# Inverse token norm held as 96 x 3 and spread by matmul, in a Nystrom attention followed by two MLPs

## The chip, the cores and the metric

One core of a Trainium2 chip runs the whole program. The metric is the device time of one execution in microseconds (us). The core has five engines that each work through their own instructions in order: TensorE (PE, its weight loads listed as PEld), VectorE (DVE), ScalarE (ACT), GpSimd (POOL) and SyncE (SP), which here issues nearly all DMAs.

## The reference

```python
def _attn_ref(q, k, v):                       # B, H, S, D = 4, 8, 576, 64
    q_lm, k_lm = ...                          # means over 18 neighbours: 32 landmarks
    A, Bm, C = sm(q, k_lm), sm(q_lm, k_lm), sm(q_lm, k)
    Z = Bm.T / (norm1 * norminf + 1e-06)
    for _ in range(6):
        Z = 2 * Z - Z @ Bm @ Z
    return A @ Z @ C @ v

def _moe_ref(x, w_gate, w_val, w_out, rms_g): # 2304 tokens, 512 -> 1536 -> 512
    rms = np.sqrt(np.mean(x * x, axis=-1, keepdims=True) + 1e-06)
    xn = x / rms * rms_g
    g = xn @ w_gate
    return g * (1 / (1 + np.exp(-g))) * (xn @ w_val) @ w_out

def _moe2_ref(x, w_in, w_out, s, b):          # 512 -> 2048 -> 512
    r = np.maximum(x @ w_in, 0.0)
    return (s * (r * r) + b) @ w_out
```

The attention's output, 512 features for each of 2304 tokens, is what `_moe_ref` calls `x`. The change touches only how `1 / rms` is formed and laid out.

## The kernel before, in words

The work is cut by batch: four batches of 576 tokens, each in two halves `hf` of `HC` = 288 tokens. For each batch `attention(b, ...)` makes the attention's factors; `fused`, `hidden` and `out_mm` then run the first MLP over twelve column blocks of its weights; the second MLP follows for all tokens at the end, from about 530 us. The first batch's attention is all that can run at the start. The attention of each later batch is spread among the MLP work of the batch before it. The int64 weights of the first MLP are loaded, narrowed to float32 on ACT and DVE by `narrow` (lines 897 to 904) and written back once in float32 during the first batch; later batches read that copy.

The order of instructions is fixed before the run by `Scheduler.run`, a planner that walks over all operations with a cost for each and a key (its due time), and gives each to an engine at the planned moment. An operation may name several engines: a pair of costs from `dp(n)` offers `t_dve(n)` on DVE and `t_pool(n)` on POOL, and within the attention an extra `SPA` = 0.5 us counts against DVE. The planner's cost of `t_dve(288)` is 0.36 us, of `t_pool(288)` 0.75 us. Once written, each engine's order is kept, whatever the real durations are. While the planner sees PE free in the first 60 planned us it fills the time with dummy matmuls (`warm`, line 1228).

The norm of a half works as follows. `x_mm` (line 821) makes the 512 features of 288 tokens in four pieces of 128 partitions by 288 tokens in PSUM, ACT squares each into `xq` with the scale 512^-0.5 (line 827), and, in later batches, two additions fold the four pieces into one (line 833). A matmul with a 128 x 128 matrix of ones (line 839) sums over the partitions and leaves the same sum in all 128 rows of `pS`: 128 x 288. The first batch accumulates its four pieces in four such matmuls instead of folding them. On `pS`, in place in PSUM, DVE adds 1e-6 (line 843) and takes the reciprocal (line 844), ACT takes the square root (line 847, for which ACT changes its table, and changes it back for the next Tanh at line 1006), and DVE multiplies the two tiles `a` of the half by it (line 852). ACT and POOL then split `a` into a high and a low part `xh`, `xl` (lines 856 and 858), the moving operand of every first matmul of that batch (line 991).

Around it, on the same engines, stands the MLP's own loop: PE makes `pU` (line 972), ACT and DVE split it into `uh`, `ul` (lines 978 and 980), PE multiplies by `xh`, `xl` (line 991), ACT takes Tanh (line 1006), and DVE makes the hidden values (lines 1008 and 1012), which free the PSUM tiles that the next line 972 and line 991 write. PE's output matmuls are lines 1035 and 1039, their operands split at lines 871 to 873.

In PSUM the later batches' attention has two banks (`at_r`), the first batch's seven (`any_r`).

Of the kernel before, what the change touches and what calls it, by code (L numbers as in the profile page):

```python
# [13 lines left out]
ACTF = mybir.ActivationFunctionType  # L14
ALU = mybir.AluOpType
# [207 lines left out]
def t_dve(n):  # L223
    return 0.065 + 0.00104 * n
# [6 lines left out]
def t_act(n):  # L231
    return 0.055 + 0.00085 * n
# [10 lines left out]
def t_mm4(n):  # L243
    return 0.00167 * max(n, 120)
# [3 lines left out]
def tile_nystrom_attention_two_mlps(  # L248
# [152 lines left out]
    def attention(b, t0, t1):  # L401
# [8 lines left out]
        def at(alts, pos, fn, r=(), w=(), pair=False):  # L410
            mine.append(op(alts, 0.0, fn, r, w, pair or set(alts) == {"dve", "pool"}))
            mine[-1].spare = {"dve": SPA if b else SPA0}
            if not first and "sp" not in mine[-1].alts:
                mine[-1].after = RELB
            at_ops.append(mine[-1])

        def dp(n):
            return {"dve": t_dve(n), "pool": t_pool(n)}
# [389 lines left out]
        for hf in range(2):  # L808
            p0 = 0.7 + 0.15 * hf
            xq = Buf(t_ring)  # L810
            n_mine = len(mine)
            for c in range(KD):
                g, pr = divmod(c, 2)
                if pr == 0:
                    pX2 = [Buf(ps_r), Buf(ps_r)]
                pX = pX2[pr]

                def x_mm(_, g=g, pX2=pX2, hf=hf):
                    for i in range(2):
                        p = slice(64 * i, 64 * i + 64)  # L820
                        nc.tensor.matmul(
                            out=pX2[i].t[:, 0:HC], lhsT=WBD.t[p, 128 * g:128 * g + 128],
                            rhs=AT[hf, g].t[p, 0:HC], start=True, stop=True)

                if pr == 0:
                    at(("pe", 0.6), p0, x_mm, r=[WBD, AT[hf, g]], w=[*pX2, (xq, "taken")])
                at(("act", t_act(HC)), p0 + 0.01, lambda e, c=c, pX=pX, xq=xq: e.activation(
                    out=xq.t[:, HC * c:HC * c + HC], in_=pX.t[:, 0:HC], func=ACTF.Square, scale=float(DM) ** -0.5),
                    r=[pX], w=[(xq, c)])
            pS = Buf(ps_r)  # L830
            if not first:
                for c, n in ((2, 2 * HC), (1, HC)):
                    at(dp(n), p0 + 0.03, lambda e, c=c, n=n, xq=xq: e.tensor_tensor(
                        out=xq.t[:, 0:n], in0=xq.t[:, 0:n], in1=xq.t[:, HC * c:HC * c + n], op=ALU.add),
                        r=[(xq, i) for i in range(KD)] if n > HC else [(xq, 0), (xq, c)],
                        w=[(xq, 0)] + ([(xq, 1)] if n > HC else []))
            n_sum = KD if first else 1
            for c in range(n_sum):
                at(("pe", t_mm4(HC)), p0 + 0.05, lambda e, c=c, pS=pS, xq=xq: nc.tensor.matmul(
                    out=pS.t[:, 0:HC], lhsT=ones, rhs=xq.t[:, HC * c:HC * c + HC],  # L840
                    start=(c == 0), stop=(c == n_sum - 1)), r=[(xq, c), "const"] + ([pS] if c else []), w=[pS])
            def s_rec(e, pS=pS):
                e.tensor_scalar(out=pS.t[:, 0:HC], in0=pS.t[:, 0:HC], scalar1=1e-6, scalar2=None, op0=ALU.add)
                e.reciprocal(out=pS.t[:, 0:HC], in_=pS.t[:, 0:HC])

            at(("dve", 2 * t_dve(HC)), p0 + 0.06, s_rec, r=[pS], w=[pS])
            at(("act", t_act(HC) if first else 1.3 + t_act(HC)), p0 + 0.07, lambda e, pS=pS: e.activation(
                out=pS.t[:, 0:HC], in_=pS.t[:, 0:HC], func=ACTF.Sqrt), r=[pS, "table"], w=[pS])
            for g in range(2):
                a = AT[hf, g]  # L850
                cols = slice(2 * HC * g + HC * hf, 2 * HC * g + HC * hf + HC)
                at(("dve", t_dve(HC)), p0 + 0.08, lambda e, a=a, pS=pS: e.tensor_tensor(
                    out=a.t[:, 0:HC], in0=a.t[:, 0:HC], in1=pS.t[:, 0:HC], op=ALU.mult), r=[a, pS], w=[a])
                wh, wl = (([(pair[i], ("a", hf, g))] + ([(pair[i], "t")] if fine else [])) for i in range(2))
                at({"act": t_act(HC), "dve": t_dve2(HC)}, p0 + 0.09, lambda e, a=a, cols=cols: (
                    e.activation(out=part(0, "t")[:, cols], in_=a.t[:, 0:HC], func=ACTF.Copy) if e is nc.scalar
                    else e.tensor_copy(out=part(0, "t")[:, cols], in_=a.t[:, 0:HC])), r=[a], w=wh, pair=True)
                at(dp(HC), p0 + 0.1, lambda e, a=a, cols=cols: e.tensor_tensor(
                    out=part(1, "t")[:, cols], in0=a.t[:, 0:HC], in1=part(0, "t")[:, cols].bitcast(F32),
                    op=ALU.subtract), r=[a, wh[0]], w=wl)  # L860
            if hf:
                late.extend(mine[n_mine:])
# [402 lines left out]
```

## Time and profile before

| what | value |
|---|---|
| median of 3 runs | 922.77 us (922.74 to 926.39) |
| the profiled execution | 924.32 us, of which its instructions span 922.3 us |
| granted TensorE clock, mean | 0.990 |
| PE busy | 881.8 us, 96% of the span |
| DVE busy | 722.4 us, 78% |
| ACT busy | 444.9 us, 48% |
| POOL busy | 124.1 us, 13% |

A busy time is a sum over the span. The share of an engine differs by stage: the attention and the first MLP fill the span up to about 530 us, the second MLP the rest, which PE fills without a gap. The chain that ended last goes back from the last instruction to what released each; over the whole span PE holds 76% of it, DVE 11%, DMA 5%.

### The profile page before, as it was taken

The page shows a single profiled execution, that of the slowest core. Times are in us where ns is not written, and L with a number is a line of the kernel's source. Part 1 is how long each engine was busy: PE and PEld are TensorE (multiplying, and loading weights), DVE is VectorE, ACT ScalarE, POOL GpSimd, SP SyncE. Part 2 cuts the span into 40 slices and gives each one's busy share as a digit, 9 for nine tenths or more (in the row PEclk, how much of TensorE's full clock was granted, in tenths as well). Part 3 has the DMA queues.
Part 4 walks back from the last instruction along what each step waited for, and adds up shares of the span by engine and source line. Part 5 has one row for each costly group of instructions (what it writes and reads, how often), then busy time and mean ns, then how long its engine had stood idle before and what let it go on. Part 6 is the DMA issues. An engine that isn't in the chain of part 4 may idle for free.

```text
span 922.3 us, 16186 instructions
## 1 busy us (share of the span) xinstructions
PE 881.8 (96%) x6077; PEld 734.5 (80%) x6077; DVE 722.4 (78%) x1454; ACT 444.9 (48%) x885; POOL 124.1 (13%) x154
## 2 busy tenths in 40 slices
PE   8778998999989999999899999999999999999998
PEld 5565766898868988798788888888888888888896
DVE  7878888887898878888989966676667666666686
ACT  5466657434553345556767333343334334333454
POOL 1550053500850004200000000000000000000000
PEclk9989998999999999999999999999999999999999
DMA  7778878873524433348876200010001000100010
GB/s 222 197 231 282 279 223 271 289 255 92 144 85 143 131 101 91 94 145 268 288 253 220 74 0 1 1 46 1 0 1 46 1 1 0 47 1 1 18 30 23
DMA packets 72126, 105.92 MB, mean 115 GB/s; under 512 B 25200, under 2 KB 45680, under 8 KB 72048
## 3 DMA queue, kind: packets, MB, share of 16 engines
q1 hardware_dynamic: 71856, 104.62, 36.2%
q8 instruction: 48, 0.79, 0.3%
q14 instruction: 30, 0.25, 0.1%
q10 hardware_dynamic: 192, 0.26, 0.1%
HBM read 90.70 MB, written 14.16 MB: 114 GB/s over the span
## 4 chain that ended last, share of the span: by engine, by line
PE 76%; DVE 11%; DMA 5%; issue 3%; ACT 3%; SPq 0%; DVEq 0%; ACTq 0%
PE bank L1065 21%; PE bank L955 21%; PE bank L991 13%; PE bank L1039 10%; PE bank L972 3%; DVE cmag L901 2%; DMA stage<-in_moe_w_val_dram 2%; PE bank L1035 2%; DMA stage<-in_moe_w_out_dram 1%; PE bank L642 1%; PE bank L1228 1%; PE bank L580 1%; DVE wl L873 1%; DMA region<-in_q_dram 1%; DVE rawg L904 1%
## 5 line engine op out<-in xcount | busy, mean ns | idle before, releaser
L991 PE MATMUL bank<-xh,uh 128*128 128x288 f32 x384 | 127.1, 331 | 14.6 <-DVE ul L980 12.9
L955 PE MATMUL bank<-xh,uh 128*128 128x512 f32 (+1 forms) x320 | 117.7, 368 | 1.0 <-ACT hbuf L1206 1.0
L955 PE MATMUL bank<-xl,uh 128*128 128x512 f32 (+1 forms) x320 | 117.6, 368 | 0.0
L955 PE MATMUL bank<-xh,ul 128*128 128x512 f32 (+1 forms) x320 | 117.6, 368 | 0.0
L1206 ACT ACTIVATE hbuf<-bank 128x512 f32<-128x512 f32 (+1 forms) x79 | 44.0, 556 | 149.5 <-PE bank L955 147.5
L991 PE MATMUL bank<-xl,uh 128*128 128x288 f32 x384 | 114.5, 298 | 0.0
L991 PE MATMUL bank<-xh,ul 128*128 128x288 f32 x384 | 114.4, 298 | 0.0
L1065 PE MATMUL bank<-wh,hh 128*128 128x512 f32 x288 | 112.4, 390 | 0.3 <-DVE hh L872 0.3
L1065 PE MATMUL bank<-wl,hh 128*128 128x512 f32 x288 | 112.3, 390 | 0.0
L1065 PE MATMUL bank<-wh,hl 128*128 128x512 f32 x288 | 112.0, 389 | 0.0
L991 PEld LDWEIGHTS bank<-xh,uh 128*128 128x128 f32 x384 | 73.3, 191 | 40.1 <-DVE ul L980 16.8
L1039 PE MATMUL bank<-hh,wh 128*128 128x288 f32 x336 | 101.1, 301 | 0.0
L1039 PE MATMUL bank<-hl,wh 128*128 128x288 f32 x336 | 99.6, 296 | 1.0 <-DVE hl L873 1.0
L1039 PE MATMUL bank<-hh,wl 128*128 128x288 f32 x336 | 99.0, 295 | 0.0
L873 DVE TENSOR_TENSOR hl<-hbuf,hh 128x512 fp32r<-128x512 f32 (+2 forms) x126 | 73.6, 585 | 2.4
L991 PEld LDWEIGHTS bank<-xl,uh 128*128 128x128 f32 x384 | 73.7, 192 | 0.7
L991 PEld LDWEIGHTS bank<-xh,ul 128*128 128x128 f32 x384 | 73.5, 191 | 0.0
L955 PEld LDWEIGHTS bank<-xh,uh 128*128 128x128 f32 x320 | 60.2, 188 | 12.6 <-ACT hbuf L1206 1.2
L955 PEld LDWEIGHTS bank<-xl,uh 128*128 128x128 f32 x320 | 60.0, 188 | 11.0
L872 DVE CAST uh<-region 128x512 fp32r<-128x512 f32 x57 | 24.3, 426 | 56.7 <-PE bank L955 56.7
L955 PEld LDWEIGHTS bank<-xh,ul 128*128 128x128 f32 x320 | 60.1, 188 | 10.0
L1039 PEld LDWEIGHTS bank<-hh,wh 128*128 128x128 f32 x336 | 63.2, 188 | 3.6 <-issue 2.1
(188 smaller groups left out, 1849.0 us busy)
## 6 DMA issues: line engine op xcount, KB each, us to landing
rawo<-kepto SPq DMA_DIRECT2D x84, 256.0 KB, 3.3
rawg<-keptg SPq DMA_DIRECT2D x36, 512.0 KB, 3.7
stage<-in_moe_w_out_dram SPq DMA_DIRECT2D x28, 512.0 KB, 4.9
stage<-in_moe_w_in_dram SPq DMA_DIRECT2D x16, 512.0 KB, 5.4
stage<-in_moe_w_gate_dram SPq DMA_DIRECT2D x12, 512.0 KB, 4.9
stage<-in_moe_w_val_dram SPq DMA_DIRECT2D x12, 512.0 KB, 5.4
keptg<-rawg SPq DMA_DIRECT2D x12, 512.0 KB, 6.2
region<-in_k_dram SPq DMA_DIRECT2D x8, 576.0 KB, 5.8
```

The costliest lines, as they stand in the source:

```text
L580: nc.tensor.matmul(out=ps.t[p, pn * g:pn * g + n], lhsT=lhsT(p, g), rhs=rhs(p, g), start=True, stop=True)
L642: nc.tensor.matmul(out=ps.t[:, 0:HC], lhsT=part(u, "bd")[:, 128 * e:128 * e + 128], rhs=part(y, "t").rearrange("p (t e i) -> p t e i", e=2 ...
L872: else e.tensor_copy(out=hi(), in_=src())), r=r, w=[wh], pair=True)
L873: b = op({"dve": t_dve(n), "pool": t_pool(n)}, key, lambda e: e.tensor_tensor(out=lo(), in0=src(), in1=hi().bitcast(F32), op=ALU.subtract) ...
L901: op(("dve", t_dve(512)), key, lambda e: e.scalar_tensor_tensor(out=m.t, in0=word(1), scalar=-2 ** 31, in1=m.t, op0=ALU.bitwise_and, op1=A ...
L955: nc.tensor.matmul(out=ps.t[:, 0:n], lhsT=w[a].t[:, ks], rhs=x[y].t[:, kd, 0:n], start=(kd == 0 and i == 0), stop=(kd == KD - 1 and i == 2))
L972: nc.tensor.matmul(out=pU.t[64 * i:64 * i + 64, 256 * g:256 * g + 256], lhsT=gw[b].t[:, 64 * k:64 * k + 64], rhs=r.t[:, :, 128 * k:128 * k ...
L991: nc.tensor.matmul(out=ps.t[:, 0:HC], lhsT=u[a].t[:, 256 * g + 128 * part:256 * g + 128 * part + 128], rhs=x[y].t.rearrange("p k n -> p (k ...
L1035: nc.tensor.matmul(out=A[c].t[:, 0:HC], lhsT=r.t[:, 128 * c:128 * c + 128], rhs=h.t, start=(f == 0), stop=(f == F1 - 1))
L1039: nc.tensor.matmul(out=A[c].t[:, 0:HC], lhsT=w[a].t[:, 128 * c:128 * c + 128], rhs=hs[y].t[:, 0:HC], start=(f == 0 and i == 0), stop=(f == ...
L1065: nc.tensor.matmul(out=A[c].t, lhsT=hs[a].t[:, s], rhs=w[y].t, start=(f == 0 and i == 0), stop=(f == F2 - 1 and i == 2))
L1206: e.activation(out=r.t[:, 0:n], in_=ps.t[:, 0:n], func=ACTF.Relu) if e is nc.scalar
```

## The change

The square's scale is dropped and comes back as 1/512 in the small addition. The sum over features is taken the other way round: `xq`, 96 tokens at a time, is the stationary operand and one column of ones the moving one, so that the sums of a half lie in PSUM as 96 partitions by 3 columns (`NP` = 96). DVE scales, adds and takes the reciprocal of these 96 x 3 values into an SBUF tile `rs`, ACT takes the square root there. DVE or POOL multiplies an identity of 96 x 96, repeated three times, by the three columns: `dg`, 96 x 288, three diagonal blocks. A matmul of 96 x 128 ones with `dg` spreads the values over all 128 partitions of a new PSUM tile `pR`, by which the two tiles `a` are multiplied as before. The costs given to the planner change with it.

```diff
-                    ... func=ACTF.Square, scale=float(DM) ** -0.5),
+                    ... func=ACTF.Square), r=[pX], w=[(xq, c)])
-            pS = Buf(ps_r)
+            pS, pR, rs, dg = Buf(ps_r), Buf(ps_r), Buf(sm_r), Buf(a_ring)
...
-            for c in range(n_sum):
-                at(("pe", t_mm4(HC)), p0 + 0.05, lambda e, c=c, pS=pS, xq=xq: nc.tensor.matmul(
-                    out=pS.t[:, 0:HC], lhsT=ones, rhs=xq.t[:, HC * c:HC * c + HC], ...
-            def s_rec(e, pS=pS):
-                e.tensor_scalar(out=pS.t[:, 0:HC], in0=pS.t[:, 0:HC], scalar1=1e-6, ...
-                e.reciprocal(out=pS.t[:, 0:HC], in_=pS.t[:, 0:HC])
-            at(("dve", 2 * t_dve(HC)), p0 + 0.06, s_rec, r=[pS], w=[pS])
-            at(("act", t_act(HC) if first else 1.3 + t_act(HC)), p0 + 0.07, lambda e, pS=pS: e.activation(
-                out=pS.t[:, 0:HC], in_=pS.t[:, 0:HC], func=ACTF.Sqrt), r=[pS, "table"], w=[pS])
+            def s_mm(_, pS=pS, xq=xq):
+                for j in range(3):
+                    for c in range(n_sum):
+                        nc.tensor.matmul(
+                            out=pS.t[0:NP, j:j + 1], lhsT=xq.t[:, HC * c + NP * j:HC * c + NP * j + NP],
+                            rhs=ones[:, 0:1], start=(c == 0), stop=(c == n_sum - 1))
+            at(("pe", 0.26 * n_sum), p0 + 0.05, s_mm, ...)
+            def s_rec(e, pS=pS, rs=rs):
+                e.tensor_scalar(out=rs.t[0:NP, 0:3], in0=pS.t[0:NP, 0:3], scalar1=1.0 / DM, scalar2=1e-6, ...)
+                e.reciprocal(out=rs.t[0:NP, 0:3], in_=rs.t[0:NP, 0:3])
+            at(("dve", 0.3), p0 + 0.06, s_rec, r=[pS], w=[rs])
+            at(("act", 0.2 if first else 1.4), p0 + 0.07, lambda e, rs=rs: e.activation(
+                out=rs.t[0:NP, 0:3], in_=rs.t[0:NP, 0:3], func=ACTF.Sqrt), r=[rs, "table"], w=[rs])
+            at(dp(HC), p0 + 0.07, lambda e, rs=rs, dg=dg: e.tensor_tensor(
+                out=dg.t[0:NP]..., in0=ident[0:NP, 0:NP]... , in1=rs.t[0:NP, 0:3]... , op=ALU.mult), ...)
+            at(("pe", t_mm4(HC)), p0 + 0.08, lambda e, dg=dg, pR=pR: nc.tensor.matmul(
+                out=pR.t[:, 0:HC], lhsT=ones[0:NP, :], rhs=dg.t[0:NP], start=True, stop=True), ...)
...
-                    out=a.t[:, 0:HC], in0=a.t[:, 0:HC], in1=pS.t[:, 0:HC], op=ALU.mult), r=[a, pS], w=[a])
+                    out=a.t[:, 0:HC], in0=a.t[:, 0:HC], in1=pR.t[:, 0:HC], op=ALU.mult), r=[a, pR], w=[a])
```

## Rows read from the trace of the kernel before

**Rows 1.** The page, part 1: busy us, share of the span, instructions.

```profile
PE 881.8 (96%) x6077; PEld 734.5 (80%) x6077; DVE 722.4 (78%) x1454; ACT 444.9 (48%) x885; POOL 124.1 (13%) x154
```

**Rows 2.** Stretches: length, busy PE, PEld, DVE, ACT, POOL; clock, DMA share, GB/s.

```profile
40.00:50.00 10.00, 3.54 (x24) 2.25 (x23) 8.80 (x13) 4.09 (x11) 2.31 (x3) 0.86 0.84 244
140.00:150.00 10.00, 7.06 (x37) 4.72 (x35) 9.76 (x13) 6.67 (x11) 3.08 (x5) 0.98 0.87 300
...
180.00:190.00 10.00, 10.00 (x77) 9.28 (x75) 7.58 (x16) 4.24 (x9) 0.97 (x1) 1.00 0.85 297
260.00:270.00 10.00, 7.11 (x51) 6.01 (x49) 9.82 (x16) 7.20 (x13) 2.22 (x3) 1.00 0.23 72
380.00:390.00 10.00, 8.57 (x72) 7.28 (x72) 8.36 (x21) 5.25 (x11) 3.93 (x4) 1.00 0.35 98
...
150.60:157.00 6.40, 6.36 (x34) 5.66 (x34) 5.58 (x12) 6.34 (x11) 1.14 (x2) 0.55 0.70 204
```

**Rows 3.** Groups by shape: busy us, mean ns | idle before, releasers.

```profile
L844 DVE RECIPROCAL bank<-bank 128x288 f32<-128x288 f32 x8 | 15.7, 1966 | 0.3
L843 DVE TENSOR_SCALAR bank<-bank 128x288 f32<-128x288 f32 x8 | 3.5, 440 | 2.0 <-PE bank L839 2.0
L758 DVE RECIPROCAL region<-region 128x9 f32<-128x9 f32 x16 | 3.5, 216 | 0.5
L852 DVE TENSOR_TENSOR region<-region,bank 128x288 f32<-128x288 f32 x16 | 6.4, 447 | 0.3 <-ACT bank L847 0.2
L761 POOL TENSOR_TENSOR region<-region 128x288 f32<-128x288 f32 x14 | 9.9, 704 | 15.4 <-ACT ca L897 7.5 <-DVE region L758 6.0 <-ACT region L708 0.6
L839 PEld LDWEIGHTS bank<-region,ones 128*128 128x128 f32 x20 | 3.5, 189 | 0.9 <-POOL region L833 0.3
```

**Rows 4.** Timeline, second batch's norm: start us, us, instruction [idle before <-releaser].

```profile
145.75 0.68 ACT L897 ACTIVATE ca<-stage 128x512 f32<-128x512 f32 x1 [3.29 <-DMA stage<-in_moe_w_gate_dram]
146.71 1.97 DVE L844 RECIPROCAL bank<-bank 128x288 f32<-128x288 f32 x1
146.88 0.58 ACT L978 ACTIVATE uh<-bank 128x512 fp32r<-128x512 f32 x1
149.91 0.69 DVE L980 TENSOR_TENSOR ul<-bank,uh 128x512 fp32r<-128x512 f32 x1
150.65 0.61 PE L991 MATMUL bank<-xh,uh 128*128 128x288 f32 x1 [3.59 <-DVE ul L980]
```

**Rows 5.** Timeline, third batch's norm.

```profile
263.23 0.41 ACT L1006 ACTIVATE hbuf<-bank 128x288 f32<-128x288 f32 x1
265.83 0.45 DVE L1008 SCALAR_TENSOR_TENSOR hbuf<-hbuf,bank 128x288 f32<-128x288 f32 x1
266.34 1.08 PE L972 MATMUL bank<-rawg,gw 128*64 128x256 f32 x8 [2.50 <-DVE hbuf L1008]
```

**Rows 6.** Timeline, fourth batch's norm.

```profile
378.10 0.41 ACT L1006 ACTIVATE hbuf<-bank 128x288 f32<-128x288 f32 x1
379.77 0.44 DVE L1008 SCALAR_TENSOR_TENSOR hbuf<-hbuf,bank 128x288 f32<-128x288 f32 x1
380.27 1.08 PE L972 MATMUL bank<-rawg,gw 128*64 128x256 f32 x8 [1.04 <-DVE hbuf L1008]
```

**Rows 7.** The chain that ended last, one of its DMA pieces: start us, us.

```profile
79.22 6.43 DMA stage<-in_moe_w_gate_dram
```

**Rows 8.** Timeline, first batch: the weight conversion behind the norm.

```profile
46.30 0.66 ACT L897 ACTIVATE ca<-stage 128x512 f32<-128x512 f32 x1 [2.57 <-DMA stage<-in_moe_w_val_dram]
49.10 0.70 DVE L901 SCALAR_TENSOR_TENSOR cmag<-stage,cmag 128x512 int32<-128x512 int32 x1
```

**Rows 9.** Timeline, PE weight loads of narrow matmuls, eight merged in each row.

```profile
206.17 0.97 PEld L555 LDWEIGHTS bank<-region 128*128 128x128 f32 x8
230.88 0.63 PEld L972 LDWEIGHTS bank<-rawg,gw 128*64 128x64 f32 x8 [0.16 <-issue]
```

**Rows 10.** Timeline, one DVE instruction of 288 columns beside a POOL instruction.

```profile
255.61 1.67 DVE L873 TENSOR_TENSOR hl<-hbuf,hh 128x288 fp32r<-128x288 f32 x1
```

More of the change, by code (lines that the diff above doesn't have):

```diff
@@ L827, in attention @@
                 at(("act", t_act(HC)), p0 + 0.01, lambda e, c=c, pX=pX, xq=xq: e.activation(
-                    out=xq.t[:, HC * c:HC * c + HC], in_=pX.t[:, 0:HC], func=ACTF.Square, scale=float(DM) ** -0.5),
-                    r=[pX], w=[(xq, c)])
-            pS = Buf(ps_r)
+                    out=xq.t[:, HC * c:HC * c + HC], in_=pX.t[:, 0:HC], func=ACTF.Square), r=[pX], w=[(xq, c)])
+            pS, pR, rs, dg = Buf(ps_r), Buf(ps_r), Buf(sm_r), Buf(a_ring)
             if not first:
@@ L837, in attention @@
             n_sum = KD if first else 1
-            for c in range(n_sum):
-                at(("pe", t_mm4(HC)), p0 + 0.05, lambda e, c=c, pS=pS, xq=xq: nc.tensor.matmul(
-                    out=pS.t[:, 0:HC], lhsT=ones, rhs=xq.t[:, HC * c:HC * c + HC],
-                    start=(c == 0), stop=(c == n_sum - 1)), r=[(xq, c), "const"] + ([pS] if c else []), w=[pS])
-            def s_rec(e, pS=pS):
-                e.tensor_scalar(out=pS.t[:, 0:HC], in0=pS.t[:, 0:HC], scalar1=1e-6, scalar2=None, op0=ALU.add)
-                e.reciprocal(out=pS.t[:, 0:HC], in_=pS.t[:, 0:HC])
@@ new lines, in attention @@
+            at(("pe", 0.26 * n_sum), p0 + 0.05, s_mm, r=[*[(xq, c) for c in range(n_sum)], "const"], w=[pS])
+            def s_rec(e, pS=pS, rs=rs):
+                e.tensor_scalar(out=rs.t[0:NP, 0:3], in0=pS.t[0:NP, 0:3], scalar1=1.0 / DM, scalar2=1e-6, op0=ALU.mult, op1=ALU.add)
+                e.reciprocal(out=rs.t[0:NP, 0:3], in_=rs.t[0:NP, 0:3])
+            at(("dve", 0.3), p0 + 0.06, s_rec, r=[pS], w=[rs])
+            at(("act", 0.2 if first else 1.4), p0 + 0.07, lambda e, rs=rs: e.activation(
+                out=rs.t[0:NP, 0:3], in_=rs.t[0:NP, 0:3], func=ACTF.Sqrt), r=[rs, "table"], w=[rs])
@@ new lines, in attention @@
+            at(dp(HC), p0 + 0.07, lambda e, rs=rs, dg=dg: e.tensor_tensor(
+                out=dg.t[0:NP].rearrange("p (j c) -> p j c", j=3),
+                in0=ident[0:NP, 0:NP].unsqueeze(1).to_broadcast([NP, 3, NP]),
+                in1=rs.t[0:NP, 0:3].rearrange("p (j o) -> p j o", o=1).to_broadcast([NP, 3, NP]),
+                op=ALU.mult), r=[rs, "ident"], w=[dg])
+            at(("pe", t_mm4(HC)), p0 + 0.08, lambda e, dg=dg, pR=pR: nc.tensor.matmul(
+                out=pR.t[:, 0:HC], lhsT=ones[0:NP, :], rhs=dg.t[0:NP], start=True, stop=True),
+                r=[dg, "const"], w=[pR])
@@ L851, in attention @@
                 cols = slice(2 * HC * g + HC * hf, 2 * HC * g + HC * hf + HC)
-                at(("dve", t_dve(HC)), p0 + 0.08, lambda e, a=a, pS=pS: e.tensor_tensor(
-                    out=a.t[:, 0:HC], in0=a.t[:, 0:HC], in1=pS.t[:, 0:HC], op=ALU.mult), r=[a, pS], w=[a])
+                at(("dve", t_dve(HC)), p0 + 0.08, lambda e, a=a, pR=pR: e.tensor_tensor(
+                    out=a.t[:, 0:HC], in0=a.t[:, 0:HC], in1=pR.t[:, 0:HC], op=ALU.mult), r=[a, pR], w=[a])
                 wh, wl = (([(pair[i], ("a", hf, g))] + ([(pair[i], "t")] if fine else [])) for i in range(2))
```

## The prediction

> **What bounds the kernel now.** I read the page first: PE is busy for 96% of the span [rows 1], so only what makes PE wait, or adds to its work, can move the end. The stretches of ten us then show where PE is not full. In most of the first MLP it is, as in the stretch from 180 us, where it is busy for all 10.00 us while DVE has time over [rows 2]; from 530 us on it is full too, and the change doesn't reach there. The exceptions that lie at a norm are four: 6.46 us of PE idle in 40 to 50 us (first batch), 2.94 us from 140 (second), 2.89 us from 260 (third), 1.43 us from 380 (fourth); in the middle two DVE is busy for 9.76 and 9.82 of 10 us [rows 2]. There DVE is late and PE waits for it. The second batch's gap costs twice: over the 6.40 us after it, in which PE is busy again, the granted clock is 0.55, that is mostly the lower level of 1.2 GHz instead of 2.4 [rows 2].
>
> The groups by shape say why DVE is late just there: the reciprocal of 128 x 288 takes 1.966 us, and the addition ahead of it 0.440, eight times each [rows 3]. The planner was told 0.73 us for both together, a third of the 2.41 us that they take, so that all that it put behind them on DVE comes about 1.7 us later than planned, and twice that where both halves follow each other.
>
> **The change, part by part.** I sum against the profiled execution (924.32 us: a span of 922.3 and 2.0 around it), which is 1.55 us above the median.
>
> *DVE gets time back.* Two instructions of 2.41 us become two on 96 x 3 values. A reciprocal of nine columns took 0.216 [rows 3]; so the pair costs 0.43 at most. About 2.0 us go per half, 16 in all. What that is worth is read stage by stage, from the row on which PE waited:
> - Second batch. PE's first matmul at 150.65 has waited 3.59 us for the DVE split at 149.91, whose input ACT delivers at 146.88 + 0.58 = 147.46. In between DVE runs the second reciprocal (146.71 to 148.68) and two weight conversions [rows 4]. Without it the split could run from 147.5 to 148.15 and PE from 148.2: 2.4 us gained, after which ACT is late next, since it had waited 3.29 us for a weight DMA [rows 4]. A gap of about 1.2 us is left. In this trace gaps of 2.50 and 1.04 us [rows 5, 6] stand in stretches whose clock stays at 1.00 [rows 2], so I take the loss at the lower clock as gone: 0.45 x 6.40 = 2.9 us. Together 5.3, with 2.4 and 6.5 as its ends (the clock drops all the same; the whole gap goes).
> - Third batch. PE's line 972 at 266.34 waits for line 1008 at 265.83, though its Tanh ended at 263.23 + 0.41 = 263.64 [rows 5]; the second reciprocal and the two multiplications behind it lie between. With DVE free it ends at 264.1: 2.2 us.
> - Fourth batch. The same pair: Tanh ends at 378.51, line 1008 begins at 379.77 and PE at 380.27 after 1.04 us of waiting [rows 6]. 1.0 us.
> - First batch. The largest gap is worth the least, I think. What follows it is paced by loading and narrowing the int64 weights, whose DMAs carry the chain (one piece is 6.43 us [rows 7]). The weights land at 46.30; ACT's two conversions of 0.66 could be done by 47.65, but DVE takes up its part at 49.10, behind the norm [rows 8]. I give 1.4 us, with ends of -1.4 (PE's new small matmuls and the longer way through `dg` hold up the first matmul) and 6.5 (the whole gap).
>
> Sum of the gains: 5.3 + 2.2 + 1.0 + 1.4 = 9.9 us.
>
> *PE gets more work.* The matmul that spreads `dg` has the 288 columns of the one that it replaces, so in later batches these two cancel. New are three products with one moving column. They are float32, which the trace shows as two weight loads for each, so six loads per half. No row has a load of 96 columns: eight of 128 columns take 0.97 us, eight of 64 columns 0.63 [rows 9], 0.121 and 0.079 each. I take 0.10, between them, which is 0.6 us per half and 3.6 us for the six later halves (2.8 to 4.4 by the two rows). In the third and fourth batch they fall right into the stage in which PE waits for DVE anyhow, so I count half, 1.8; if that cover is gone it is 3.6. In the first batch four 288-column matmuls per half make way for twelve narrow ones and one wide, inside the 6.46 us of idle PE, at no price of their own.
>
> This speaks against the change: a product with one column isn't cheap, as it pays for the stationary side. The Trainium skill says the same (TensorE: Matmul & The Clock Gate, section LDWEIGHTS): a load takes its count of columns over 1.2 GHz, whatever the number of partitions, which would be an estimate of 80 ns for 96 columns and 2.9 us instead of 3.6. The two rows agree that columns count, and stand above it.
>
> *A new wait on PE.* Before, nothing on PE waited for the root; now the spreading matmul does, through `dg`, and PE's queue is in order: whatever stands behind it, the next batch of first and output matmuls, waits too. The bound from below is nothing, if the planner's distance holds; from above one ACT delay of 3.29 us [rows 4] per half. The nearest row is the old sum over partitions, also a matmul at the end of a chain through ACT, DVE and POOL: its loads were preceded by 0.9 us of idle PE in all, mostly not its input's doing [rows 3]. Spread over six later halves that is 0.15 each, and I take it again: 0.9 us.
>
> *The diagonal.* 96 x 288 values from two SBUF inputs: 0.447 us on DVE or 0.704 on POOL by the same shape [rows 3]. With 0.5 us counted against DVE the planner will often choose POOL, which has time (13% busy [rows 1]). On DVE it would take back 0.45 of each 2.0 us, which the waits priced above still leave room for. So it costs nothing in the sum; if the cover goes, on DVE 0.45 us per half, or what rival 2 has on POOL. ACT's root shrinks a little, its table changes remain, no DMA is moved: nothing either.
>
> Net: 9.9 - 1.8 - 0.9 = 7.2 us, so 917.1 beside the profiled execution, and **915.6 us** beside the median.
>
> **The rivals.**
> 1. *More comes back.* A late DVE shifts everything behind it, and I priced one wait per batch only. If all four gaps went (6.46 + 2.94 + 2.89 + 1.43 = 13.7) with the 2.9 of clock, less 2.7, it would be 924.3 - 13.9 - 1.55 = 908.8. For it: DVE at 98% in these stretches. Against it: the weight DMAs in the first batch. I expect 907 to 912.
> 2. *The gain is given back on DVE.* When POOL holds the diagonal, a DVE instruction beside it can be blocked: one of 288 columns took 1.67 us beside a POOL instruction [rows 10], where a two-input one of that size takes 0.447 [rows 3]. At 1.2 us for each of six later halves, 7.3 us are lost at the very place of the gain: 915.6 + 7.3 = 922.9. Against it: POOL's new instruction is short, and DVE need not have a two-input one from SBUF at that moment. The Trainium skill has this as a rule (SBUF — State Buffer, section SBUF: two separate sides): the two engines share a port pair as an exclusive lock, held for a whole instruction. The 1.67 us [rows 10] agree with it.
> 3. *Slower.* The new wait on PE is the mechanism, in the norms of the first and second batch, where ACT's queue holds weight conversions that wait for DMAs the planner took to be earlier. A root behind one of these stops PE itself. At 2 us for each of eight halves it is 915.6 - 0.9 + 16 = 930.7. It decides from a mean wait of about 1.0 us: eight times that is all of the net gain. For it: the 3.29 us and 2.57 us that ACT stood still [rows 4, 8]. Against it: such waits don't stand in the third and fourth batch, where the weights come as float32.
>
> The planner works with other costs, so its whole order may move a little; that widens each case rather than making one.
>
> **How the numbers follow.** My forecast (912 to 918) gets 0.40, rival 1 0.22, rival 2, with other ways to end near no change, 0.22, rival 3 0.16. A measurement of this kernel can tell about 0.5%, 4.6 us, from no change: under 918.2 is faster, 0.62; up to 927.4 the same, 0.22; above it slower, 0.16. The range goes from 907, the near end of rival 1, to 926, which takes in rival 2 and leaves most of rival 3 out.
>
> **What would show it.** Right: line 844's 15.7 us nearly vanish from the groups, the 3.59, 2.50 and 1.04 us waits shrink or go, the clock from 150 to 157 us stays at 1.00, and PE's busy time rises by some 3 to 4 us. Wrong: PE idle time that is released by DVE's or POOL's `dg` (rival 3), DVE instructions of over 1 us beside POOL's new line (rival 2), or waits that come back at other places of the first MLP because something else, the weight DMAs or ACT, was as late as DVE.

## The result and the profile after

The changed kernel takes 911.06 us (median of four runs, 910.41 to 912.77), beside 923.7 us for the kernel before (four runs). The ratio is 0.9877, with a 95% interval of 0.9854 to 0.9900: faster by 1.2%, some 12 us. The prediction was 915.6 us with a range of 907 to 926. The profiled execution, the longest of the four, took 912.77 us; its instructions span 910.8 us, and the mean granted clock is 0.992.

The first view is the page of the kernel after, part 1: busy us, share of the span, instructions.

```profile
PE 883.3 (97%) x6145; PEld 738.0 (81%) x6145; DVE 707.9 (78%) x1458; ACT 439.5 (48%) x881; POOL 127.2 (14%) x160
```

Beside [rows 1], PE is busy for 1.5 us more and DVE for 14.5 us less. The span is PE's busy time and its idle time: 881.8 + 40.5 us before, 883.3 + 27.5 us after. So 13.0 us of idle PE went and 1.5 us of busy PE came: 11.5 us. The 1.5 us is a balance. The norm's own products (line 839 before, 841 and 859 after) went from 9.3 to 15.2 us of PE, and the matmuls on `xh` and `xl` (line 991 before, 1004 after) from 356.0 to 351.0 us for the same count, as several of their stretches now have a higher clock.

The second view is the groups by shape of the kernel after: busy us, mean ns, then the idle time before them with its releaser. Line 841 is the narrow product, 848 and 849 the small addition and reciprocal, 854 `dg`, 859 the spreading matmul, 865 the multiplication of `a`.

```profile
L841 PEld LDWEIGHTS bank<-ones,region 128*96 128x96 f32 x60 | 7.3, 200 | 1.0 <-POOL region L832 0.8
L865 DVE TENSOR_TENSOR region<-region,bank 128x288 f32<-128x288 f32 x16 | 6.7, 449 | 3.5 <-PE bank L859 3.4
L854 POOL TENSOR_TENSOR region<-ident,region 96x288 f32<-96x288 f32 x7 | 5.1, 732 | 15.5 <-ACT region L852 15.5
...
L849 DVE RECIPROCAL region<-region 96x3 f32<-96x3 f32 x8 | 1.4, 172 | 0.3
L848 DVE TENSOR_SCALAR region<-bank 96x3 f32<-96x3 f32 x8 | 1.2, 154 | 6.4 <-PE bank L841 6.4
```

The pair on DVE fell from 2.41 us [rows 3] to 0.154 + 0.172 = 0.33 us: 16.6 us in all. POOL took the diagonals, at 0.73 us.

The third view is the stretches of the kernel after, with the columns of [rows 2].

```profile
40.00:50.00 10.00, 8.74 (x49) 6.37 (x49) 3.99 (x10) 4.53 (x12) 5.45 (x8) 0.70 0.73 222
140.00:150.00 10.00, 8.87 (x60) 6.80 (x60) 9.69 (x19) 6.64 (x14) 2.23 (x4) 1.00 1.01 344
150.00:160.00 10.00, 7.54 (x37) 5.64 (x34) 8.78 (x13) 4.15 (x9) 8.33 (x9) 0.83 0.78 274
...
180.00:190.00 10.00, 8.96 (x66) 7.94 (x65) 7.34 (x16) 3.65 (x8) 0.00 (x0) 1.00 0.86 276
...
260.00:270.00 10.00, 9.76 (x82) 8.12 (x82) 8.86 (x21) 5.46 (x14) 8.53 (x12) 1.00 0.35 112
380.00:390.00 10.00, 10.00 (x77) 8.98 (x77) 7.89 (x20) 2.31 (x5) 0.00 (x0) 1.00 0.41 132
```

PE's idle time went from 6.46 to 1.26 us in the first batch's stretch, from 2.89 to 0.24 in the third's, from 1.43 to nothing in the fourth's. In the second batch it went from 2.94 to 1.13 in one stretch, but the stretch behind it, from 150 us, now has 2.46. In the kernel before that one reads:

```profile
150.00:160.00 10.00, 9.36 (x53) 7.50 (x54) 8.83 (x19) 8.99 (x17) 3.90 (x5) 0.68 0.75 235
```

There PE was idle for 0.64 us, at a clock of 0.68, which is now 0.83. Over the two stretches together PE is idle for 3.58 us before and 3.59 after: in this execution the second batch's wait has moved and not gone.

How far the kernel after is ahead at a given place is read from the start of the first matmul on `xh` (line 991 before, 1004 after) of each column block and batch. The time before less the time after:

| place (start before, us) | lead, us | second execution |
|---|---|---|
| first batch, block 0 (54.3) | 0.9 | 0.4 |
| first batch, block 5 (93.8) | 6.7 | 6.5 |
| first batch, block 8 (125.4) | 6.8 | 5.4 |
| block 9 (138.6) | 5.5 | 4.2 |
| block 10 (152.8), behind the wait of [rows 4] | 9.6 | 8.3 |
| block 12, behind the second batch's norm | 4.8 | 6.5 |
| block 20 (249.0) | 2.4 | 4.2 |
| block 23 (281.1), behind the third norm | 6.6 | 8.5 |
| block 32 (365.6) | 5.9 | 7.8 |
| block 34 (386.2), behind the fourth norm | 8.2 | 10.1 |
| block 38 (417.1) | 8.3 | 10.1 |
| block 44 (469.7) | 11.8 | 13.8 |
| end of the span | 11.5 | 13.3 |

The last column is a second profiled execution of the same changed kernel (run beside one of the experiments), against the same execution of before. Its steps from row to row agree with the first's within some 0.3 us, but for two: from block 5 to 8 nothing is lost in one and 1.1 us in the other, and from block 10 to 12 it is 4.8 us in one and 1.8 in the other. Over the second batch's norm as a whole, from block 5 to 12, 1.9 us are lost in one and nothing in the other.

### The profile page after: what moved, and what is told of

Read it like the earlier page. It is cut to its first block, busy times and chain, and to the rows that moved or that the text cites. A ratio compares the mean times of both kernels' runs of the same rounds, so it can differ in the third digit from the quotient of the medians.

```text
span 910.8 us, 16338 instructions
## 1 busy us (share of the span) xinstructions
PE 883.3 (97%) x6145; PEld 738.0 (81%) x6145; DVE 707.9 (78%) x1458; ACT 439.5 (48%) x881; POOL 127.2 (14%) x160
## 4 chain that ended last, share of the span: by engine, by line
PE 78%; DVE 12%; DMA 3%; issue 3%; ACT 2%; SPq 1%; DVEq 0%; ACTq 0%
PE bank L1078 21%; PE bank L968 21%; PE bank L1004 13%; PE bank L1052 11%; PE bank L985 4%; DVE cmag L914 2%; PE bank L1048 2%; DMA stage<-in_moe_w_gate_dram 2%; DVE wl L886 2%; PE bank L642 1%; PE bank L821 1%; DMA region<-in_q_dram 1%; PE bank L841 1%; DVE ul L993 1%; DVE hbuf L1021 1%
## 5 line engine op out<-in xcount | busy, mean ns | idle before, releaser
L1004 PE MATMUL bank<-xh,uh 128*128 128x288 f32 x384 | 124.6, 324 | 7.5 <-DVE ul L993 6.6
L1004 PEld LDWEIGHTS bank<-xh,uh 128*128 128x128 f32 x384 | 72.2, 188 | 33.4 <-DVE ul L993 11.8
L886 DVE TENSOR_TENSOR wl<-rawo,wh 128x512 fp32r<-128x512 f32 x84 | 62.7, 748 | 11.5 <-ACT wh L884 7.5
```

The source lines that it names most:

```text
L886: b = op({"dve": t_dve(n), "pool": t_pool(n)}, key, lambda e: e.tensor_tensor(out=lo(), in0=src(), in1=hi().bitcast(F32), op=ALU.subtract) ...
L1004: nc.tensor.matmul(out=ps.t[:, 0:HC], lhsT=u[a].t[:, 256 * g + 128 * part:256 * g + 128 * part + 128], rhs=x[y].t.rearrange("p k n -> p (k ...
```

## Experiments

Two theories stood against each other. By the first, called D here, DVE's time at the norms is what was gained. By the second, the planner, which got new operations and new costs, only happened on a better order. Where the gain of the second batch went had its own question: the DMAs of the weights (W), or DVE and POOL.

**DVE's work put back into the changed kernel.** A scratch tile `old` of 128 x 272 is added to and inverted behind the small reciprocal, with the order of the changed kernel kept.

```diff
                 e.reciprocal(out=rs.t[0:NP, 0:3], in_=rs.t[0:NP, 0:3])
+                e.tensor_scalar(out=old, in0=old, scalar1=1e-6, scalar2=None, op0=ALU.add)
+                e.reciprocal(out=old, in_=old)
```

> The changed kernel, with an addition and a reciprocal of 128 x 272 on a scratch tile put behind the two small DVE instructions of each half. The planner isn't told, so every engine's order is that of the changed kernel; nothing waits for the scratch result but what stands behind it on DVE. Theory D (the gain is DVE's time, 2.0 us per half): the gain goes, 920 to 926 us. Theory O (the gain is another order of the plan, with the new costs): it stays, 911 to 913 us.

Measured: 922.53 us beside 922.86, ratio 0.9993 [0.9980, 1.0007]. The whole gain is gone. Its groups by shape, then its waits of PE from 140 to 400 us (total us, times, longest):

```profile
L853 DVE RECIPROCAL old<-old 128x272 f32<-128x272 f32 x8 | 14.8, 1853 | 0.3
L852 DVE TENSOR_SCALAR old<-old 128x272 f32<-128x272 f32 x8 | 2.3, 291 | 0.0
```

```profile
PE bank L1008 <- DVE ul L997: 7.1, 5, 2.8
PE bank L1052 <- DVE rawo L921: 2.6, 2, 2.5
```

17.1 us of DVE time, whose result nothing reads, bring back PE's waits on the split `ul`, 7.1 us of them, as [rows 4] had one. All else of the change is still there, so without DVE's time it pays nothing. The waits are not the whole of the loss:

```profile
PE 891.0 (97%) x6145; PEld 744.9 (81%) x6145; DVE 723.4 (78%) x1475; ACT 441.0 (48%) x881; POOL 126.4 (14%) x160
```

The span is 922.1 us, so PE is idle for 31.1 us, 3.6 more than in the changed kernel, but busy for 7.7 us more with the same 6145 matmuls. The granted clock, 0.983 on the mean beside 0.992, falls in the stretches of the late norms: 0.87 from 260 to 270 us and 0.77 from 370 to 380, where the changed kernel has 1.00. By these rows a late DVE can cost twice, as a wait and once more as clock.

**The planner told the truth.** The kernel before, with the pair's real cost.

```diff
-            at(("dve", 2 * t_dve(HC)), p0 + 0.06, s_rec, r=[pS], w=[pS])
+            at(("dve", 2.4), p0 + 0.06, s_rec, r=[pS], w=[pS])
```

> The kernel before, with one number changed: the planner is told 2.4 us for the addition and the reciprocal instead of 0.73. No work is taken away. Theory D: DVE has as much to do, 919 to 925 us. Theory P (what hurt was that the planner did not know of the 2.4 us, so PE's order was wrong there): most of the gain comes without the change, 911 to 915 us.

Measured: 921.41 us, ratio 0.9980 [0.9966, 0.9995]. To know the real cost is worth some 0.2%; the time itself has to go.

**The time alone taken away.** The kernel before without its reciprocal (it leaves out the inversion; order and all other operations are those of before).

```diff
                 e.tensor_scalar(out=pS.t[:, 0:HC], in0=pS.t[:, 0:HC], scalar1=1e-6, ...
-                e.reciprocal(out=pS.t[:, 0:HC], in_=pS.t[:, 0:HC])
```

> The kernel before without the reciprocal of 128 x 288 (the values are then not inverted), with the planner's costs as before, so each engine's order is that of the kernel before. 1.97 us go from DVE eight times, with no new matmul, no diagonal and no new wait. Theory D: 910 to 914 us, at least as good as the changed kernel, since PE has nothing added. Theory O: 920 to 924 us.

Measured: 913.5 us, ratio 0.9898 [0.9879, 0.9917]: 1.0 of the 1.2%, with before's order. Together with the first run this settles for D: with DVE's time back in the new order the gain is gone, with it out of the old order most of the gain is there.

This run also shows what is late next in the second batch. Its timeline there (start us, us, instruction, idle before):

```profile
142.34 0.66 ACT L896 ACTIVATE ca<-stage 128x512 f32<-128x512 f32 x1 [2.71 <-DMA stage<-in_moe_w_gate_dram]
143.47 0.58 ACT L977 ACTIVATE uh<-bank 128x512 fp32r<-128x512 f32 x1
143.60 0.69 DVE L900 SCALAR_TENSOR_TENSOR cmag<-stage,cmag 128x512 int32<-128x512 int32 x1 [2.58 <-ACT cmag L898]
144.93 0.68 DVE L979 TENSOR_TENSOR ul<-bank,uh 128x512 fp32r<-128x512 f32 x1
145.67 0.41 PE L990 MATMUL bank<-xh,uh 128*128 128x288 f32 x1 [2.13 <-DVE ul L979]
```

ACT stands for 2.71 us on a weight DMA, so its high part `uh` comes late (143.47 + 0.58 = 144.05), and so do the two weight conversions that stand ahead of the split on DVE and need ACT too; the split `ul` starts at 144.93, and PE still waits 2.13 us. The prediction had named this wait of ACT [rows 4] as the next one.

**The change in the first batch alone, and in the later three alone.** The new code under `if first:`, or under `if not first:`, and the old code for the other batches.

> The change in the first batch alone; the three later ones as before. Read from the start of each unit of the first MLP, the changed kernel is 6.7 us ahead by its sixth unit, at 87 us, of 11.7 at the end: by that the first batch alone gives 915 to 918 us. My prediction priced the first batch at 1.4 us, which would be 921 to 923 us.

> The change in the three later batches alone; the first as before. By the units' starts the first batch's part is worth 6.7 of the 11.7 us of the full change, the rest 5: 916 to 919 us if the stages are independent. If the later batches' DVE time is worth as much as my prediction gave it (8.5 us gross, 5.8 net): 915 to 918. If all of the gain hangs on the first batch: 921 to 924.

Measured: 919.7 us, 0.9967 [0.9947, 0.9988], for the first batch; 917.95 us, 0.9945 [0.9917, 0.9972], for the others. By their medians that is 3.2 and 5.9 us, 9.1 together, where both at once gave 12.6. The intervals are too wide to say that the parts do not add up, but one row shows a reason why they need not. The waits of PE from 140 to 165 us where only the first batch is changed:

```profile
PE bank L1022 <- DVE hbuf L1043: 3.9, 1, 3.9
```

This kernel was 11.1 us ahead at block 10 and 4.9 at block 11. Here part of what the first batch gains is lost again, where the second batch's two long reciprocals are still in the way of PE.

**Half the bytes of the first MLP's weights.** In the changed kernel the int64 tiles are loaded half (the other half of the weights is left out, a constant stands in its place).

```diff
+        n_in = 256 if kind == 1 else 512
-                e.dma_start(out=st.t, in_=wt[c, :])
+                e.dma_start(out=st.t[:, 0:n_in], in_=wt[c, 0:n_in])
```

> The changed kernel, of which the first MLP loads only half of each of its int64 weight tiles (the other half of the tile is a constant, so the outputs are not those of the reference); every instruction on the engines stays, and the orders are those of the changed kernel. Theory W (after the change the weight DMAs and the conversions that wait for them hold the stretch up to about 160 us, which is why the lead of the first batch shrinks and the second batch gains nothing): 904 to 908 us. Rival: the conversions on DVE beside POOL, not the DMAs, hold it: 910 to 912 us.

Measured: 910.29 us, 0.9874 [0.9837, 0.9912], the same as the changed kernel. Its waits of PE from 140 to 165 us:

```profile
PE bank L1051 <- DVE rawo L920: 2.7, 2, 2.5
```

The wait of 2.5 us stands where it stood, so W falls for this place: the DMAs of the weights don't hold the second batch's norm of the changed kernel. Elsewhere they do hold PE: from 80 to 90 us PE is idle for 0.67 us, where the changed kernel has 1.73, and of the changed kernel's two waits from 155 to 235 us (0.65 and 0.39 us) none is left. By the medians all this is worth no more than the noise.

**The diagonal on DVE only.**

```diff
-            at(dp(HC), p0 + 0.07, lambda e, rs=rs, dg=dg: e.tensor_tensor(
+            at(("dve", t_dve(HC)), p0 + 0.07, lambda e, rs=rs, dg=dg: e.tensor_tensor(
```

> The changed kernel with the diagonal offered to DVE alone. In the changed kernel all eight stand on POOL, 0.66 us each. Rival 2 of my prediction (on POOL it blocks DVE by the shared port): 908 to 910 us, faster by more than the 0.45 us that DVE takes per half. Otherwise DVE has 3.6 us more to do and its share of the gain goes, a quarter to a fifth: 913 to 915 us.

Measured: 917.03 us, 0.9940 [0.9915, 0.9964], slower than the changed kernel. That was a miss in size: it lost more than was expected. Its group by shape:

```profile
L854 DVE TENSOR_TENSOR region<-ident,region 96x288 f32<-96x288 f32 x7 | 3.0, 441 | 0.3 <-ACT region L852 0.3
```

Eight instructions of 0.441 us are 3.5 us of DVE, and by the ratios (0.9940 - 0.9877 = 0.0063) some 6 us are lost, though the ends of the two intervals are only 0.0015 apart. So POOL is the better place for `dg`, and the prediction's second rival, that POOL's diagonal would cost DVE the gain, is refuted. Why the loss is larger than the work was not found; the planner's order changed too. In the profiled execution (914.58 us) it lies in the first batch: the lead is 3.9 us at block 5, where the changed kernel has 6.7, and 7.3 at block 23, where it has 6.6.

**A short POOL instruction at the second batch's norm, and the changed kernel once more.** In the landmark sums of the later batches' attention, POOL's addition of 576 columns (line 482) is cut to 64 (it leaves out the rest of these sums). There are twelve such additions, from 30 to 268 us, and one of them stands at the second batch's norm. The changed kernel itself was run beside it, since this asks for less than 1%.

```diff
-                    out=y(), in0=x()[:, 0:9], in1=x()[:, 9:18], op=ALU.add), ...
+                    out=y()[:, 0:1], in0=x()[:, 0:1], in1=x()[:, 9:10], op=ALU.add), ...
```

> The changed kernel in whose later batches POOL's first addition of the segment sums (line 482) runs over 64 columns instead of 576, so that those batches' means are of a part of their tokens only; planner costs and orders are as in the changed kernel. Beside that addition two weight conversions on DVE took 1.30 and 1.78 us in the second batch's stage instead of 0.69, and PE waited 2.46 us for the second of them. Theory N (after the change DVE instructions blocked by POOL are what is late next in the second batch's stage): the 2.46 us wait goes, with it the lower clock behind it, 905 to 908 us. Rival (the wait has another cause): 910 to 912 us and the wait still there.

> The changed kernel once more, as the measure for the runs beside it: 910 to 912 us.

Measured: 908.84 us (908.06 to 909.22) beside 912.11 us (910.93 to 914.87) for the changed kernel; ratios to before 0.9845 [0.9809, 0.9881] and 0.9885 [0.9845, 0.9926]. First the timeline of the changed kernel's first profiled execution, from its second batch:

```profile
150.77 1.30 DVE L914 SCALAR_TENSOR_TENSOR cmag<-stage,cmag 128x512 int32<-128x512 int32 x1
151.48 1.85 POOL L482 TENSOR_TENSOR region<-region 128x576 f32<-128x576 f32 x1
152.10 1.78 DVE L917 SCALAR_TENSOR_TENSOR rawo<-ca,cmag 128x512 int32<-128x512 int32 x1
153.93 0.75 PE L1048 MATMUL bank<-hbuf,rawo 128*128 128x288 f32 x2 [2.46 <-DVE rawo L917]
```

PE now waits for the conversion of the output weights. It takes 1.78 us beside POOL's 1.85 us. With POOL's instruction cut, the timeline of the same place is:

```profile
152.18 0.69 DVE L917 SCALAR_TENSOR_TENSOR rawo<-ca,cmag 128x512 int32<-128x512 int32 x1
152.93 0.75 PE L1048 MATMUL bank<-hbuf,rawo 128*128 128x288 f32 x2 [1.38 <-DVE rawo L917]
```

and in the second execution of the changed kernel itself:

```profile
152.71 1.17 DVE L917 SCALAR_TENSOR_TENSOR rawo<-ca,cmag 128x512 int32<-128x512 int32 x1
153.93 0.75 PE L1048 MATMUL bank<-hbuf,rawo 128*128 128x288 f32 x2 [1.25 <-DVE rawo L917]
```

The conversion falls to 0.69 us when POOL is short, and no run of the one kernel lies within those of the other. But the intervals of the two ratios overlap, and the wait of the unchanged second execution is as short. So POOL's neighbourhood is supported as the reason that the conversion is slow, but the 3.3 us are not made at this place: beside the second execution the light kernel is ahead by 1.3 us at block 0 already, by 1.0 at block 12 and by 3.2 at block 23. Which of the other eleven additions brought them was not tried.

**Only the order changed.** `MORE` is a number of the planner alone; the changed kernel with another value does the same work in another order.

```diff
-    MORE = 1.4
+    MORE = 1.2
```

> The changed kernel with the planner's spare time per unit of the first MLP (MORE) at 1.2 us instead of 1.4, since DVE has 2.0 us less to do per half. If the spare time was there for DVE, 908 to 911 us; if the due times don't set the order where PE waits, 911 to 914.

Measured: 917.76 us, 0.9950 [0.9924, 0.9976], 5.6 us slower than the changed kernel on the same chip. Its waits of PE from 130 to 170 us:

```profile
PE bank L1048 <- DVE rawo L917: 2.7, 2, 1.7
PE bank L859 <- POOL region L854: 1.8, 1, 1.8
```

The second row is the spreading matmul that waits for `dg`: the mechanism of the prediction's third rival, once, at 1.8 us. In the changed kernel's own order no wait on line 859 stands among those of PE in the norms of the later batches. So the order alone can move this kernel by some half of what the change brought, and a part of the 12 us may be the luck of this order; the second theory is wrong as the main cause, not as a cause.

## Why the prediction was right, point by point

**The bound, DVE late at the norms: right for the later batches.** Shown by the runs with the reciprocal put back and taken out. The 98% of DVE that rival 1 reads hold for the second and third batch alone; in the first and fourth DVE is busy for 8.80 and 8.36 of 10 us [rows 2].

**Third and fourth batch: the mechanism right, the terms too small.** The 2.50 and 1.04 us waits [rows 5, 6] are gone. The waits of PE in the kernel after, from 245 to 395 us, are now small:

```profile
PE bank L1004 <- DVE ul L993: 0.5, 2, 0.3
PE bank L985 <- DVE hbuf L1021: 0.2, 1, 0.2
```

The terms were 2.2 and 1.0 us. The lead rose by 4.2 us from block 20 to 23, where PE's idle time from 245 to 285 us fell from 4.88 to 0.74 us, and by 2.3 us from block 32 to 34, in both executions. One wait for each batch had been priced; others near it went too, as rival 1 said. Not all of them were the reciprocal's: the largest, 0.94 us in the third batch, ends at 257.94 us, before the first half's reciprocal starts at 258.66, and without reciprocals but with before's order it is still there. That run gains 3.1 and 1.7 us at these two norms; what the changed kernel has above them, 1.1 and 0.6, goes with the new order.

**Second batch: the largest term, 5.3 us, and it failed.** The 3.59 us wait [rows 4] is gone as foretold, and from block 9 to 10 the lead rises by 4.1 us in both executions; but from block 10 to 12 it falls by 4.8 and 1.8 us, so that over the whole norm, from block 5 to 12, it fell by 1.9 us in one execution and stayed as it was in the other. The step that failed is "ACT is late next", with 1.2 us left of the gap. Next to be late was DVE again, with the conversion of the output weights (2.46 us of waiting, 1.25 in the second execution), behind a stretch in which DVE is still busy for 9.69 of 10 us. With before's order the run without reciprocals shows ACT late next, as predicted, but with 2.13 us of gap: the reading of [rows 4] had left out that the two weight conversions ahead of the split wait for ACT too. Of the 2.9 us of clock some came back: from 150 to 160 us it is 0.83 in the first execution, behind the wait of 2.46 us, and 1.00 in the second, behind 1.25 us; before it was 0.68. In the next 70 us, to block 20, which the sum had left out, another 2.4 us of lead went (2.3 in the second execution); 1.04 us of that is idle time of PE from 180 to 190 us, where before was full [rows 2]. The larger part of it stands behind ACT, which had waited for a DMA of the output weights:

```profile
184.03 0.67 ACT L910 ACTIVATE ca<-stage 128x512 f32<-128x512 f32 x1 [3.69 <-DMA stage<-in_moe_w_out_dram]
186.74 1.08 PE L985 MATMUL bank<-rawg,gw 128*64 128x256 f32 x8 [0.65 <-DVE hbuf L1021]
```

This is a wait of the kind that the prediction's last paragraph names as a sign of being wrong, and with half the bytes it doesn't stand there. The rest was not traced.

**First batch: 1.4 us was far too little.** By block 5 the lead is 6.7 us (6.5 in the second execution), near the upper end (6.5) that the prediction had named and set aside because of the weight DMAs. The kernel after, ACT's timeline in the first batch, and PE's first matmul on `xh`:

```profile
39.42 0.20 ACT L852 ACTIVATE region<-region 96x3 f32<-96x3 f32 x1 [1.85 <-DVE region L849]
42.96 0.20 ACT L852 ACTIVATE region<-region 96x3 f32<-96x3 f32 x1 [3.34 <-DVE region L849]
47.33 0.67 ACT L910 ACTIVATE ca<-stage 128x512 f32<-128x512 f32 x1
53.43 0.38 PE L1004 MATMUL bank<-xh,uh 128*128 128x288 f32 x1
```

Both roots now stand ahead of the weight conversion (line 910), which had waited for its DMA until 46.30 [rows 8]. PE's 6.46 us of idle time there became 1.26. At block 0 little of that is ahead (0.9 us), since PE filled the time with narrow products at a low clock (last section) and with dummy matmuls. The rest came in two stretches, of which the kernel before has

```profile
50.00:60.00 10.00, 9.42 (x62) 6.83 (x61) 6.27 (x7) 4.36 (x8) 5.61 (x7) 0.80 0.61 182
...
80.00:90.00 10.00, 6.50 (x59) 4.55 (x60) 7.40 (x17) 6.17 (x16) 0.00 (x0) 1.00 0.79 254
```

and the kernel after

```profile
50.00:60.00 10.00, 9.75 (x83) 8.35 (x82) 8.53 (x11) 7.99 (x15) 9.29 (x12) 1.00 0.89 288
...
80.00:90.00 10.00, 8.27 (x52) 6.08 (x52) 8.55 (x17) 5.72 (x12) 0.00 (x0) 1.00 0.93 282
```

The clock behind the gap was 0.80 and is 1.00: 2 us, a cost that I had seen behind the second batch's gap and not looked for behind this one. And from 80 us, where the chain runs through a weight DMA [rows 7], PE's idle time went from 3.50 to 1.73 us: the DMAs move more from 50 to 60 us (288 GB/s for 182), so that they too are ahead. I read this so: they pace this stretch, as the prediction had it, but had themselves been held up by the norm, and that was the error in setting the upper end aside. The run with half the bytes agrees with the first part (0.67 us of idle PE from 80 to 90 us, a lead of 8.6 us at block 5), but it lightens the DMAs everywhere; that the norm had held them up is argued and not shown.

Here order and time can't be parted: with DVE's work put back and the new order kept the lead at block 5 is 6.8 us, and with before's order and no reciprocals it is 4.7. Either does it. The two runs have one thing in common: in both the root no longer waits for a long reciprocal. In the first the long pair stands behind the small one, and its roots start at 37.89 and 41.72 us, where before they start at 43.34 and 46.87. So in this batch the shorter chain to the root may be the gain, and DVE's busy time nothing; no run tells these apart. What the first experiment lost, it lost later: from block 5 to the end its lead goes from 6.8 to 0.2 us.

**A term that wasn't there: the end of the first MLP.** From block 38 to 44 the lead rises by 3.5 us, in a stretch without a norm, for which the sum had nothing. The new order with DVE's work put back shows 1.8 us there and the old order without reciprocals 1.6, so each alone has about half of it. The traces show two parts. Before, PE waits there for 1.45 and 0.67 us (at 433.48 and 435.21 us), which it no longer does. And both kernels then have the same wait for `ul`, 1.75 us before 459.70 and 1.76 us before 449.49, but what follows it differs. The kernel before, then the kernel after:

```profile
460.00:470.00 10.00, 10.00 (x65) 9.30 (x64) 8.66 (x19) 5.04 (x11) 0.00 (x0) 0.83 0.86 278
450.00:460.00 10.00, 10.00 (x77) 9.31 (x76) 9.90 (x21) 6.52 (x15) 0.00 (x0) 1.00 0.95 319
```

That is some 1.7 us of clock. The run with DVE's work put back (460 to 470 us) and the run without reciprocals (450 to 460) have the 0.83 too. So the prediction's inference that the clock holds behind a short gap, drawn from two gaps, is not safe: here the same gap has 0.83 behind it in one kernel and 1.00 in the other. What in the planner takes the two waits away stays open.

**PE's new products: the price right.** Six loads of 96 columns were priced at 0.6 us for each half. The timeline of a later norm shows them at 0.58 and 0.63 us, 0.10 for each:

```profile
364.86 0.58 PEld L841 LDWEIGHTS bank<-ones,region 128*96 128x96 f32 x6 [0.38 <-POOL region L832]
366.93 0.63 PEld L841 LDWEIGHTS bank<-ones,region 128*96 128x96 f32 x6
```

In the second batch they take 0.74 and 0.75, so that the six later halves sum to 3.9 us, beside 3.6 priced. The prediction's sign, that PE's busy time rises by 3 to 4 us, did not come: it rose by 1.5 us. The norm's own products rose by more, 5.9 us, those of the first batch included, which the prediction had given no price, and the matmuls on `xh` and `xl` fell by 5.0. How much of the 3.6 us lay under PE's waits, for which 1.8 were taken off, was not measured. The Trainium skill's rule (TensorE: Matmul & The Clock Gate, section LDWEIGHTS) that a load takes its count of columns over 1.2 GHz would give an estimate of 80 ns; the 0.10 us measured lie above it, as the neighbouring rows had.

**The new wait of PE: 0.9 us priced, nothing found** in the profiled order. Rival 3 needs a mean wait of 1.0 us on each of eight halves. It is a real mechanism, seen once in another order, and the distances that the planner leaves for `dg` cover it here. The row behind the 0.9 us counts more than the later halves: of its 20 loads [rows 3] eight are the first batch's.

**Rival 2: not at its place.** No gain was lost beside POOL's new line, and `dg` is better off on POOL. Yet older POOL instructions stretched DVE conversions at the place of the gain: from 0.69 to 1.78 us beside the addition of line 482, and from 0.69 to 1.30 us beside a split of `a` on POOL (line 871), which stayed at 1.30 when that addition was cut. The Trainium skill (SBUF — State Buffer, section SBUF: two separate sides) tells of a port pair that one of the two engines holds for a whole instruction; the 1.78 us beside 1.85 us of POOL, and the 0.69 us once POOL is short, agree with it.

In sum, by the first execution: 6.7 us in the first batch, -1.9 from there to behind the second norm (in the second execution nothing), -2.4 behind it, 4.2 at the third, 2.3 at the fourth, 3.5 at the end of the first MLP, -0.9 elsewhere, 11.5 us together. PE's costs are in these already. The forecast had 1.4, 5.3, nothing, 2.2, 1.0, nothing, less 2.7 for PE: 7.2. The time lay in the range because the misses went both ways.

## What to carry to other kernels

An instruction on 128 x 288 values that all rows hold alike can be done on 96 x 3 values and spread by a matmul; that pays where the engine is late and PE has room, and here it took 16.6 us from DVE, put 5.9 us on PE and still gained. Before a wait is priced as gained, look for all that is late by the same cause, and for the instruction that stands next on the same engine, since it can be the next to be late; and look at the clock behind the wait, since the two can cost about as much. Where a planner fixes the order, put the old cost back into the new order, and take it out of the old one: the two runs tell the work from the order.

## What the hardware showed that I had not expected

PE lost the full clock while it was busy with products of one moving column. The stretches of the kernel after, in the first batch's norm (columns as in [rows 2]):

```profile
36.80:38.80 2.00, 2.00 (x25) 2.00 (x24) 0.36 (x2) 0.77 (x3) 0.00 (x0) 1.00 0.48 105
38.80:42.40 3.60, 3.60 (x29) 3.58 (x28) 0.33 (x2) 0.20 (x1) 0.66 (x1) 0.56 0.62 154
42.40:47.00 4.60, 4.02 (x16) 2.23 (x16) 1.67 (x5) 1.52 (x5) 2.66 (x4) 0.60 0.98 297
```

PE is busy for all of the 3.60 us from 38.80, behind 2.00 us of narrow products at full clock, and its granted clock is 0.56, mostly the lower level of 1.2 GHz. The narrow products of the first half, at the full clock, and those of the second, at mostly the lower, in the timeline:

```profile
36.78 2.12 PEld L841 LDWEIGHTS bank<-ones,xbuf 128*96 128x96 f32 x24 [0.38 <-DVE gw L802]
38.82 3.39 PEld L841 LDWEIGHTS bank<-ones,region 128*96 128x96 f32 x23
```

24 loads take 2.12 us on one level, 23 take 3.39 on the other. The second execution has it too (24 in 3.96 us). The run with the change in the first batch alone has the same products at the full clock in both halves; there the clock falls only behind them:

```profile
35.32 2.12 PEld L845 LDWEIGHTS bank<-ones,xbuf 128*96 128x96 f32 x24 [0.38 <-DVE gw L802]
37.35 2.12 PEld L845 LDWEIGHTS bank<-ones,region 128*96 128x96 f32 x24
```

That kernel is 4.1 us ahead at block 0 and 9.8 at block 5, where the changed kernel is ahead by 0.9 and 6.7. So the lower clock may cost some 3 us here, a price that busy time doesn't show; as the orders of the two kernels differ as well, this is not shown.

A reciprocal is dear by its columns, not by its start: 1.966 us for 288 columns on 128 partitions in PSUM and 0.216 for nine in SBUF [rows 3], 0.172 for three on 96 partitions.
